# Paced units, and the two sums of a gate as accumulating transfers, in a fused linear-attention and MoE kernel

## The chip, the cores and the metric

The kernel runs on one core of one Trainium2 chip. The time is the device time of one execution in microseconds (us); lower is better. A core has five engines with a queue each, worked off in order: TensorE (PE; its weight loads are PEld), VectorE (DVE), ScalarE (ACT), GpSimd (POOL) and SyncE (SP). SP and POOL issue the transfers, which 16 DMA engines carry out.

## The reference

`q, k, v, a_re, a_im` have the shape (4, 8, 768, 48). For each of the 32 pairs of batch and head a complex state S (48 x 48) is carried over 768 steps, and its output goes through a mixture of eight experts.

```python
mag = np.sqrt(a_re * a_re + a_im * a_im)
scale = np.minimum(mag, 0.999) / (mag + 1e-06)
a_re_n, a_im_n = a_re * scale, a_im * scale
for t in range(S):
    ar, ai = a_re_n[:, :, t, :, None], a_im_n[:, :, t, :, None]
    new_re = ar * S_re - ai * S_im
    new_im = ar * S_im + ai * S_re
    S_re, S_im = new_re + einsum('bhd,bhe->bhde', k[:, :, t], v[:, :, t]), new_im
    y[:, :, t] = einsum('bhd,bhde->bhe', q[:, :, t], S_re)
...
x = y.transpose(0, 2, 1, 3).reshape(3072, 384)
do_compute = x @ w_skip > 0
# of the rows kept: expert e = argmax(x @ w_gate), gate_w its softmax weight
out[row] = x[row] + gate_w[row] * (np.maximum(x[row] @ w1[e], 0) @ w2[e])
# the other rows: out = x
```

## The kernel before

The 768 steps are cut into 6 chunks of 128 (`NCH`), the chunks into 3 groups of 2 (`NG`). In a group the 128 partitions hold two halves of a chunk (one runs backwards from the chunk's middle, one forwards), two chunks and 32 heads, so that one instruction serves them all.

**Gate** (`gate`, `scale`, `scale_last`). For a piece `i` of 8 of a half chunk's 64 steps (24 pieces, 8 a group, the last of a group with one step more) `a_re` and `a_im` are loaded into `ain` (four buffers) by eight transfers on SP. `scale` finds the factor that `mag` calls for: ScalarE squares both parts into `sq` (two buffers), VectorE adds the two squares (line 261), ScalarE takes Ln and Exp, VectorE forms max(l, 0) + t (line 265), ScalarE takes the last Exp, whose result is `t` (two buffers). Two VectorE products (lines 315 and 323) and a copy with changed sign on ScalarE (line 320) put the scaled `a` back into `ain`; small memsets on POOL set edge values. The last piece of all goes through `scale_last`, which has other steps.

**Chain** (`chain`). For each of a group's 65 steps two dependent VectorE instructions multiply the running product by the step's `a`: four products X (line 370), and their sums W (line 379). Each needs the one before. `cpos` counts the steps; the first of a group is a copy (line 364).

**Consume** (`consume`, `final` for the last piece). From W come weighted keys and queries `nw` and `iw` (lines 442 and 469, shared buffers, two). VectorE has five instructions for a piece, ScalarE a Square, Ln and Exp, PE four matmuls `sw`. In groups 0 and 2 PE transposes them and ScalarE copies them to `qk`; in groups 0 and 1 POOL writes some to DRAM (`kq`, line 491), for group 1 all of them (`spilled`), to be read back as `nat`.

**Unit** (`units`, `unit_at`, `unit`). For each chunk `c` and batch `b` (24 units, 8 a group): PE makes the scores `pa` of 8 heads, VectorE masks them (line 609, two instructions), the state `T` is moved on by the factor F (line 621 on VectorE, lines 632, 633 and 652 on PE), PE makes the output (lines 663, 666, 671), ScalarE copies it to `xa`, SP stores it. The scores of the next unit are issued within the present one. After the four units of a chunk a route (`route`) chooses the experts by some twenty small VectorE instructions and scatters the rows to `xs` by four indirect transfers on POOL. `weights`, `fetch`, `tokens` and `moe` then compute the experts.

**Order.** `Order` plans the sequence in which all this is written down. Each of the above is a generator that yields its VectorE time and a delay; the one with the lowest number of those that are ready goes next (`P_UNIT` 0.5, `P_ROUTE` 0.7, `P_CONSUME` 1, `P_GATE` 2, `P_WEIGHTS` 3), and a chain takes turns with them by `SHARE` and `CREDIT`. A delay is an estimate of when another engine will be done. When the program is built, a scheduler with a model of times orders each engine's instructions; what is written earlier goes first among those that the model has ready. `issue_after` pins an instruction behind another one. A gate may begin when the chain is within `AHEAD` = 2 pieces of its piece, and only after the gate before; units of a group begin when all of its pieces are consumed, beside the next group's chain (those of the last group after it).

Of the kernel before, what the change touches and what calls it, by code (L numbers as in the profile page):

```python
# [13 lines left out]
AF = mybir.ActivationFunctionType  # L14
ALU = mybir.AluOpType
# [4 lines left out]
B, H, S, D = 4, 8, 768, 48  # L20
# [3 lines left out]
HC = 64  # L24
NCH = S // C
NG = NCH // 2
# [14 lines left out]
P_UNIT, P_ROUTE, P_CONSUME, P_REST, P_GATE, P_WEIGHTS = 0.5, 0.7, 1, 1, 2, 3  # L41
# [2 lines left out]
CREDIT = 600.0  # L44
SLACK = 0.6
AHEAD = 2
FILL = 4


class Order:  # L50
# [22 lines left out]
    def add(self, prio, gen, delay=0.0):  # L73
        self.s.append([prio, self.t + delay, gen])
# [24 lines left out]
def vt(n, f=1.0):  # L99
    return (n / f + 65) / 0.96  # L100
# [8 lines left out]
class Kern:  # L109
# [140 lines left out]
    def scale(self, i, n, ain):  # L250


        V, A, o = self.nc.vector, self.nc.scalar, self.order
        sq = self.gt.tile([128, 2, n, D], F32, name=f"sq_{i}", tag="sq")
        t = self.gt.tile([128, n, D], F32, name=f"t_{i}", tag="t")
        N = n * D
        A.activation(sq.rearrange("p c j d -> p j c d"), ain[:, :, 0:2], AF.Square, scale=1.0 / 0.999)
        u, l = sq[:, 0], sq[:, 1]
        yield o.wait(0, o.act(2 * N, 1, o.t + (2500 if i else 6000)))
        with self.tc.issue_after(self.cins) if self.cpos else ExitStack():  # L260
            V.tensor_tensor(u, sq[:, 0], sq[:, 1], ALU.add)
        A.activation(l, u, AF.Ln, bias=self.tinym)
        A.activation(t, l, AF.Exp, scale=-0.5, bias=self.lnw, accum_out=self.acc[:, 1, i:i + 1])
        yield o.wait(vt(N), o.act(2 * N, 3, o.t + vt(N)))
        V.scalar_tensor_tensor(u, l, 0.0, t, ALU.max, ALU.add)
        A.activation(t, u, AF.Exp, scale=-0.5, accum_out=self.acc[:, 0, i:i + 1])
        yield o.wait(vt(N), o.act(N, 2, o.t + vt(N)))
        return t
# [32 lines left out]
    def gate(self, g, p):  # L301
        nc = self.nc
        V, A = nc.vector, nc.scalar
        n = LP + (1 if p == NP - 1 else 0)
        i = g * NP + p
        if i == 0:
            self.load_a(0)
        if i + 1 < NPC:
            self.load_a(i + 1)
        ain = self.ain[i]  # L310
        last = i == NPC - 1
        t = yield from (self.scale_last if last else self.scale)(i, n, ain)
        N = n * D
        o = self.order
        V.scalar_tensor_tensor(ain[:, :, 0], ain[:, :, 0], self.sgn, t, ALU.mult, ALU.mult)
        if p == 0:
            nc.gpsimd.memset(ain[0:64, 0, 0], 0.0)
        if n > LP:
            nc.gpsimd.memset(ain[64:128, LP, 0], 0.0)
        A.activation(ain[:, :, 2], ain[:, :, 0], AF.Copy, scale=-1.0)  # L320
        self.ready[i] = o.act(N, 1, o.t + vt(N))
        yield vt(N), 0
        V.tensor_tensor(ain[:, :, 1], ain[:, :, 1], t, ALU.mult)
        if p == 0:
            nc.gpsimd.memset(ain[0:64, 0, 1], 1.0)
        if n > LP:
            nc.gpsimd.memset(ain[64:128, LP, 1], 1.0)
        yield vt(N), 0
        self.gates_done = i + 1

    def gates(self):
        for g in range(NG):
            for p in range(NP):
                if FILL <= g * NP + p <= FILL + E:
                    self.late(g * NP + p - FILL)
                while self.cpos < (g * NP + p - AHEAD) * LP:
                    yield 0, 200
                yield from self.gate(g, p)

    def chain(self, g):  # L340
        V = self.nc.vector
# [4 lines left out]
        prev = None  # L346
        for p in range(NP):
            i = g * NP + p
            while self.gates_done <= i:
                yield 0, 100  # L350
            yield self.order.wait(0, self.ready[i])
            num, inv = self.load_qk(i)
# [347 lines left out]
    def units(self, g):  # L700
        self.nat(2 * g, 0)
        self.nat(2 * g, 1)
        self.unit_at(2 * g, 0)
        for cc in range(2):
            c = 2 * g + cc
            while self.routes_done < c - 1:
                yield 0, 200
            if c > 0:
                yield from self.make_F(c - 1)
            if not self.last(c):  # L710
                self.lg = self.rt.tile([128, B, H // 2, E + 1], F32, name=f"lg_{c}", tag="lg", bufs=2)
            self.xa = self.rt.tile([128, B, XW], F32, name=f"xa_{c}", tag="xa", bufs=2)
            self.nc.gpsimd.tensor_copy(self.xa[:, :, DM], self.tok[:, :, c])
            for b in range(B):
                yield from self.unit(c, b)
                self.units_done += 1
            if not self.last(c):
                self.routes.append((self.lg_t, self.route(c, self.lg, self.xa)))
# [153 lines left out]
    def attention(self):  # L872
        with ExitStack() as ctx:
# [11 lines left out]
            for t in self.vts + self.sts:  # L885
                nc.gpsimd.memset(t[:, :, D:64], 0.0)
            self.pr_ins, self.T2, self.ain, self.QK, self.Ew, self.T, self.pa, self.W, self.ready, self.nats, self.kqt = [{} for _ in range(11)]
            self.cpos = self.gates_done = self.cons_done = self.routes_done = self.units_done = 0
            self.rx_t = 0.0
            self.cq, self.routes = [], []  # L890
            o = self.order = Order()
# [347 lines left out]
```

## Time and profile before

| | |
|---|---|
| three runs | 530.79, 538.38, 548.51 us; median 538.38 |
| profiled execution | 534.78 us, span 533.0 us |
| busy PE, PEld | 425.7 us (80%), 371.0 us (70%) |
| busy DVE, ACT, POOL | 411.9 us (77%), 293.3 us (55%), 88.3 us (17%) |
| mean granted PE clock | 0.896 of full speed |
| moved | 85.72 MB in 160523 packets, mean 161 GB/s |

All views are of one execution. A row of instructions has its line, engine and operation, the tile written and those read, the count and the times; behind `<-` in a row of waits stands what ended the wait, then the total in us, how often, and the longest. The strips show the busy share of 40 equal slices in tenths. A row that begins with a stretch `A:B` has the busy time of each engine in it with the number of instructions, then the granted PE clock as a share of full speed, the busy share of the DMA engines, and GB/s; asked for one line alone, the busy times are that line's. PE's busy time is modelled, and a busy PE isn't PE at its peak.

### The profile page before, as it was taken

How to read it: one execution, taken by the hardware profiler on the slowest of the kernel's cores; microseconds unless marked ns; L12 is line 12 of the kernel's file. 1: busy time of each engine (PE TensorE's matmuls, PEld its weight loads, DVE VectorE, ACT ScalarE, POOL GpSimd, SP SyncE). 2: the span in 40 equal slices, each digit the busy share in tenths (PEclk: the TensorE clock that was granted, in tenths of full speed). 3: DMA queues.
4: the chain of work that ended last, by engine and by line, in shares of the span. 5: the costliest groups of instructions: out<-in, count | busy, mean ns of one | idle time of the engine just before them, and what ended most of it. 6: DMA issues, size and time to landing. Idle time of an engine off the chain costs nothing. (4 is left out here: it accounts for less than half of the span.)

```text
span 533.0 us, 10037 instructions
## 1 busy us (share of the span) xinstructions
PE 425.7 (80%) x3253; PEld 371.0 (70%) x3253; DVE 411.9 (77%) x1139; ACT 293.3 (55%) x658; POOL 88.3 (17%) x158
## 2 busy tenths in 40 slices
PE   0355545579999223799999998999999999999994
PEld 0233323468887101688878788998998999999994
DVE  2998899966998999889889848899479666866621
ACT  3657667724557555578878665432266545564420
POOL 4011111101122274000000300221211001211111
PEclk9986876577999665599999999999999999999998
DMA  4557866788878767866735515744669567656300
GB/s 86 115 110 168 196 149 159 166 158 192 227 184 205 189 168 181 178 140 154 158 83 122 139 37 164 213 110 122 209 221 302 176 235 244 215 190 216 101 20 28
DMA packets 160523, 85.72 MB, mean 161 GB/s; under 512 B 134491, under 2 KB 154463, under 8 KB 160464
## 3 DMA queue, kind: packets, MB, share of 16 engines
q1 hardware_dynamic: 155216, 70.93, 52.4%
q0 software_dynamic: 5248, 14.07, 9.1%
q8 instruction: 28, 0.46, 0.4%
q14 instruction: 31, 0.25, 0.2%
HBM read 61.84 MB, written 25.21 MB: 163 GB/s over the span
## 5 line engine op out<-in xcount | busy, mean ns | idle before, releaser
L451 PE MATMUL sw<-ws,ident 128*128 128x384 f32 x84 | 46.1, 686 | 40.5 <-ACT ws L437 40.5
L370 DVE TENSOR_TENSOR X<-W,ain 128x192 f32<-128x192 f32 x192 | 68.0, 354 | 3.6 <-ACT ain L320 0.3
L929 DVE TENSOR_TENSOR l<-r,h 128x768 fp32r<-128x768 f32 (+1 forms) x56 | 58.1, 1070 | 11.8 <-ACT h L928 11.7
L928 ACT CAST h<-r 128x768 fp32r<-128x768 f32 (+1 forms) x56 | 49.6, 924 | 22.1 <-DMA r<-in_moe_w_dram 17.0
L451 PEld LDWEIGHTS sw<-ws,ident 128*128 128x128 f32 x84 | 19.8, 262 | 54.2 <-issue 27.8
L993 PE MATMUL ph<-xh,h 128*128 128x256 f32 x192 | 53.0, 282 | 0.6 <-issue 0.6
L993 PE MATMUL ph<-xh,l 128*128 128x256 f32 x192 | 53.2, 282 | 0.0
L995 ACT ACTIVATE hh<-ph 128x256 fp32r<-128x256 f32 x64 | 23.7, 382 | 53.0 <-PE ph L993 52.9
L379 DVE TENSOR_TENSOR W<-X 128x96 f32<-128x96 f32 x192 | 48.9, 255 | 3.2
L993 PE MATMUL ph<-xl,h 128*128 128x256 f32 x192 | 51.0, 281 | 0.0
L532 PE MATMUL tp<-ident,iw 128*96 128x128 f32 x128 | 23.7, 332 | 33.1 <-DVE iw L469 32.8
L996 DVE SCALAR_TENSOR_TENSOR hl<-ph,hh 128x256 fp32r<-128x256 f32 x64 | 25.5, 419 | 28.2 <-ACT hh L995 28.2
L539 ACT COPY qk<-tp 96x256 f32<-96x256 f32 x128 | 39.9, 369 | 13.1 <-PE tp L532 12.9
L609 DVE TENSOR_TENSOR at<-pa,mask 128x512 f32<-128x512 f32 x48 | 32.8, 686 | 18.1 <-PE pa L589 18.0
L1016 PE MATMUL po<-h,hh 128*128 128x384 f32 x128 | 43.8, 342 | 0.0
L532 PEld LDWEIGHTS tp<-ident,iw 128*96 128x96 f32 x128 | 16.7, 151 | 38.5 <-issue 30.6
L1017 PE MATMUL po<-l,hh 128*128 128x384 f32 x128 | 43.3, 338 | 0.0
L732 POOL DMA_INDIRECT xs<-xa,sl x24 | 28.6, 1192 | 85.3 <-DVE l L929 24.2
L663 PE MATMUL py<-at,vt 128*64 128x128 f32 x384 | 42.0, 291 | 0.0
L1018 PE MATMUL po<-h,hl 128*128 128x384 f32 x128 | 39.5, 337 | 0.0
L589 PE MATMUL pa<-qk 96*128 96x128 f32 x256 | 37.3, 297 | 0.1
L993 PEld LDWEIGHTS ph<-xh,h 128*128 128x128 f32 x192 | 36.2, 189 | 0.8 <-issue 0.8
(225 smaller groups left out, 1070.6 us busy)
## 6 DMA issues: line engine op xcount, KB each, us to landing
r<-in_moe_w_dram SPq DMA_DIRECT2D x24, 512.0 KB, 5.2
r<-in_moe_w_dram SPq DMA_DIRECT2D x32, 384.0 KB, 4.3
nat<-kq SPq DMA_DIRECT2D x8, 768.0 KB, 5.5
kq<-nw POOLq DMA_DIRECT2D x24, 192.0 KB, 3.7
kq<-iw POOLq DMA_DIRECT2D x24, 192.0 KB, 3.1
vt<-in_v_dram SPq DMA_DIRECT2D x24, 192.0 KB, 3.0
out_dram<-xa SPq DMA_DIRECT2D x24, 192.0 KB, 2.3
ain<-in_a_re_dram SPq DMA_DIRECT2D x90, 48.0 KB, 2.8
```

Source lines behind the costliest of these rows:

```text
L370: V.tensor_tensor(X, prev.unsqueeze(1).to_broadcast([128, 2, 2, D]), windows(ain[:, j]), ALU.mult)
L379: self.cins = V.tensor_tensor(W[:, j, ::-1], X[:, :, 0], X[:, :, 1], ALU.add).ins
L451: nc.tensor.matmul(sw, self.ident, ws[:, :, c], start=(c == 0), stop=(c == 1))
L532: nc.tensor.transpose(tp[:, jj], src[:, s * 4 + jj], self.ident)
L539: nc.scalar.copy(o, tp[:, :, :, cc].rearrange("p j s b -> p b s j"))
L663: PE.matmul(py[j * 64:j * 64 + 64, hp], vt_[:, 2 * hp + j], at[:, 2 * hp + j], start=True, stop=(c == 0))
L928: nc.scalar.copy(hi[:, ks], raw)
L929: nc.vector.tensor_tensor(lo[:, ks], raw, hi[:, ks], ALU.subtract)
L993: pe = PE.matmul(ph, w[:, k, js], x[:, k], start=(n == 0), stop=(n == len(terms) - 1))
L1016: PE.matmul(po, hh[:, j, sl], w2h[:, j], start=(j == 0), stop=False)
L1017: PE.matmul(po, hh[:, j, sl], w2l[:, j], start=False, stop=False)
L1018: pe = PE.matmul(po, hl[:, j, sl], w2h[:, j], start=False, stop=(j == NF - 1))
```

## The change

There are three parts. In `scale`, pieces 3 to 22 (`SUMS` = 3) form both sums by transfers that POOL issues and that add to their destination, instead of by VectorE; a Relu on ScalarE takes the place of the max, and the planner is told of 3500 ns for each. `gates` no longer runs a gate to its end before the next: it adds each to the plan as an entry of its own, and the set `gated` takes the place of the count `gates_done`. In `units`, unit number n of a group (n = 0 to 7) isn't begun before the next chain has done 7n steps (`PACE` = 7); the units of the last group wait for the end of the last chain.

```diff
+SUMS = 3
+PACE = 7
...
     def scale(self, i, n, ain):
...
         A.activation(sq.rearrange("p c j d -> p j c d"), ain[:, :, 0:2], AF.Square, scale=1.0 / 0.999)
         u, l = sq[:, 0], sq[:, 1]
+        if i >= SUMS:
+            add = lambda x, y: self.nc.gpsimd.dma_start(x, y, accum_op=ALU.add)
+            add(u, l)
+            A.activation(l, u, AF.Ln, bias=self.tinym)
+            A.activation(t, l, AF.Exp, scale=-0.5, bias=self.lnw, accum_out=self.acc[:, 1, i:i + 1])
+            A.activation(l, l, AF.Relu)
+            yield 0, o.act(5 * N, 6) - o.t + 3500
+            add(l, t)
+            A.activation(t, l, AF.Exp, scale=-0.5, accum_out=self.acc[:, 0, i:i + 1])
+            yield 0, o.act(N, 2) - o.t + 3500
+            return t
         yield o.wait(0, o.act(2 * N, 1, o.t + (2500 if i else 6000)))
...
     def gate(self, g, p):
...
-        self.gates_done = i + 1
+        self.gated.add(i)
...
     def gates(self):
...
                 while self.cpos < (g * NP + p - AHEAD) * LP:
                     yield 0, 200
-                yield from self.gate(g, p)
+                self.order.add(P_GATE, self.gate(g, p))
+                yield 0, 0
...
     def chain(self, g):
...
-            while self.gates_done <= i:
+            while i not in self.gated:
                 yield 0, 100
...
     def units(self, g):
...
             for b in range(B):
+                while self.cpos < min((g + 1) * (HC + 1) + (cc * B + b) * PACE, NG * (HC + 1)):
+                    yield 0, 100
                 yield from self.unit(c, b)
```

More of the change, by code (lines that the diff above doesn't have):

```diff
@@ L887, in attention @@
             self.pr_ins, self.T2, self.ain, self.QK, self.Ew, self.T, self.pa, self.W, self.ready, self.nats, self.kqt = [{} for _ in range(11)]
-            self.cpos = self.gates_done = self.cons_done = self.routes_done = self.units_done = 0
+            self.gated = set()
+            self.cpos = self.cons_done = self.routes_done = self.units_done = 0
             self.rx_t = 0.0
```

## The prediction

> **What bounds the kernel now.** First the page: span, busy engines, and the strip for DMA.
>
> ```profile
> span 533.0 us, 10037 instructions
> PE 425.7 (80%) x3253; PEld 371.0 (70%) x3253; DVE 411.9 (77%) x1139; ACT 293.3 (55%) x658; POOL 88.3 (17%) x158
> DMA  4557866788878767866735515744669567656300
> ```
>
> No engine is full over the span, so I cut it at the three chains. The first copy of a chain (line 364) dates them: the last of the three stands at 195.3, and each chain's last W step ends shortly before the next one's work takes over. I take 24 to 95.4 for chain 0 (after the start-up), 95.4 to 205.2 for chain 1, 205.2 to 306.5 for chain 2, then the last units, then the experts. Columns are length, busy time of PE, PEld, DVE, ACT and POOL with counts, granted PE clock, DMA share, GB/s.
>
> ```profile
> L364 DVE COPY W<-ain x3: 204/205/209, 12.0 to 195.3; 128x96 f32<-128x96 f32 x3
> 24.00:95.40 71.40, 38.29 (x142) 25.55 (x140) 66.02 (x177) 48.43 (x128) 9.46 (x19) 0.76 0.71 158
> 95.40:205.20 109.80, 75.27 (x579) 61.24 (x578) 95.71 (x284) 58.58 (x134) 30.93 (x45) 0.78 0.79 186
> 205.20:306.50 101.30, 94.37 (x729) 74.88 (x730) 88.25 (x246) 71.19 (x169) 7.55 (x11) 0.89 0.63 141
> 388.00:533.00 145.00, 135.50 (x960) 134.24 (x958) 89.33 (x152) 68.55 (x123) 21.07 (x25) 0.98 0.54 178
> ```
>
> Chain 0 is VectorE's: 66.0 of 71.4 us. Chain 1 has 14.1 us of VectorE idle time and takes 38 us more than chain 0. Chain 2 is shared by PE (94.4 of 101.3) and VectorE (88.3). The experts are PE's, and the change doesn't touch them. In chain 1 the loss has a place; the second row of each pair below counts the W steps alone.
>
> ```profile
> 110.00:165.00 55.00, 54.48 (x463) 47.34 (x464) 43.62 (x120) 25.96 (x59) 8.87 (x15) 0.88 0.80 188
> 110.00:165.00 55.00, 6.31 (x25) 0.88 0.80 188
> 165.00:205.00 40.00, 14.40 (x87) 9.09 (x85) 38.15 (x123) 24.19 (x53) 20.30 (x27) 0.69 0.78 188
> 165.00:205.20 40.20, 7.39 (x29) 0.69 0.79 189
> DVE at L609 <- PE pa L589: 7.8, 5, 3.8
> DVE RX L621 <- ACT T L659: 1.8, 1, 1.8
> DVE sq L265 <- ACT t L263: 2.8, 4, 1.6
> ```
>
> From 110 to 165 PE is full with the eight units of group 0, and the chain makes 25 steps in 55 us (2.2 us each); afterwards it makes 29 in 40.2 us (1.4) with PE a third busy. The waits of VectorE in chain 1 are mainly for a unit's scores (7.8 us) and its state (1.8). The last row is chain 0's: the wait for the first Exp ahead of a gate's second sum.
>
> **The change part by part.**
>
> *Two sums off VectorE.* Line 261 counts the gates in each stretch; the timeline of VectorE (start, duration) prices a sum.
>
> ```profile
> 24.00:95.40 71.40, 3.91 (x7) 0.76 0.71 158
> 95.40:205.20 109.80, 4.48 (x8) 0.78 0.79 186
> 205.20:306.50 101.30, 2.75 (x5) 0.89 0.63 141
> 39.49 0.55 DVE L261 TENSOR_TENSOR sq<-sq 128x384 f32<-128x384 f32 x1
> 39.96 0.95 DVE L442 TENSOR_TENSOR nw<-num,W 128x768 f32<-128x768 f32 x1
> 41.21 0.26 DVE L379 TENSOR_TENSOR W<-X 128x96 f32<-128x96 f32 x1
> 41.51 0.36 DVE L370 TENSOR_TENSOR X<-W,ain 128x192 f32<-128x192 f32 x1
> 46.63 0.25 DVE L379 TENSOR_TENSOR W<-X 128x96 f32<-128x96 f32 x1
> 46.80 0.55 DVE L323 TENSOR_TENSOR ain<-ain,t 128x384 f32<-128x384 f32 x1
> ```
>
> A sum holds the engine from 39.49 to 39.96, 0.47 us. But it is a filler between dependent steps: W followed by its own X takes 41.21 to 41.51, 0.30 us; with a filler behind it the engine is free again after 46.63 to 46.80, 0.17. So about 0.12 us of each sum is hidden now, and taking it out gives 0.35, or 0.70 a gate. Chain 0: 7 gates, 4.9 us, and the 2.8 us of waits at line 265 go with the instruction. Chain 1: 8 gates, 5.6. Chain 2: 5 gates, 3.5 at most; PE is 93% busy there, so I count half, 1.8. What is late next is line 315, which waits for `t`, now behind two transfers.
>
> *Units one by one.* The work of a unit doesn't change: eight score products and the other matmuls, the copies on ScalarE, on SP a load of `vt`, one of `nat` and a store of `out`, and after four units a route with four scatters on POOL. In chain 1 all of it moves from 25 steps to 56 (eight units, 7 steps apart), past loads of `ain`, `num` and `inv` on SP that keep their number. PE's 75.3 us fit beside a chain of 95, and the scores of unit b+1 are issued with unit b, 7 steps before they are read: I take away the waits for scores and state, 9.6 us, and keep the other 4.5 us of idle time. For chain 2 the row of line 609 counts the score instructions that fall inside it:
>
> ```profile
> 205.20:306.50 101.30, 8.27 (x12) 0.89 0.63 141
> ```
>
> Twelve are six units of the eight, over the chain's 65 steps, so more than 7 steps apart already; the limit moves little: 0. The units of group 2 wait for the chain's end either way.
>
> VectorE alone would then need 71.4 - 4.9 - 2.8 = 63.7 us for chain 0 and 109.8 - 5.6 - 9.6 = 94.6 for chain 1, together 158.3 instead of 181.2.
>
> *Forty accumulating transfers.* Nothing like them is in this trace, so bounds. They move 192 KB from SBUF to SBUF on POOL's queue. The nearest rows are POOL's own 192 KB writes to DRAM; and the SP queue's best stretch, with the experts' weights.
>
> ```profile
> kq<-iw POOLq DMA_DIRECT2D x7, 192.0 KB, 2.7
> kq<-nw POOLq DMA_DIRECT2D x7, 192.0 KB, 3.6
> q0 software_dynamic: 734, 2.61, 15.3%
> kq<-iw POOLq DMA_DIRECT2D x15, 192.0 KB, 3.4
> kq<-nw POOLq DMA_DIRECT2D x16, 192.0 KB, 3.9
> 400.00:420.00 20.00, 18.72 (x135) 18.50 (x135) 15.14 (x33) 12.49 (x20) 2.41 (x3) 1.00 0.74 247
> ```
>
> In chain 0, 14 writes (2.61 MB) take 15.3% of 71.4 us: 0.78 us of all 16 engines each. At the rate of 400 to 420 (0.74 of 20 us for 4.94 MB, 3.0 us a MB) 192 KB would be 0.59. An addition has to read what it adds to as well, so up to twice: 0.59 to 1.56, never below nothing. I take 1.0, the middle in ratio, since no row is nearer. Chains 0 and 1 hold 30 of them. Their DMA work now is 0.71 x 71.4 + 0.79 x 109.8 = 137.4 us of all 16 engines; with 30 it is 167.4. That is more than VectorE's 158.3: **the transfers become the later end in the two chains.** By 0.59 the sum is 155.1 and VectorE decides, by 1.56 it is 184.2 and nothing is left. The Trainium skill (DMA: Bandwidth & Descriptors, Rules for kernel authors) says that an accumulating transfer reads its destination and writes it later; by that rule the price lies towards the upper end, which no row here can show.
>
> In time, a transfer lands 2.7 to 3.9 us after its issue, and POOL's issue is in order: behind an addition that waits for ScalarE stand the `kq` writes, whose landing frees `nw` and `iw`, and the memsets of `ain`. POOL is busy 9.5 of 71.4 us, so I put 0 on its time.
>
> *ScalarE.* One Relu a gate, 0.53 us by the row of line 266, 3.7 us in chain 0: 52 of 64, hidden while it isn't full. The waits for landings are the rival below.
>
> ```profile
> L266 ACT ACTIVATE t<-sq 128x384 f32<-128x384 f32 (+1 forms) x6 | 3.2, 528 | 3.2 <-DVE sq L265 3.2
> L257 ACT ACTIVATE sq<-ain 128x768 f32<-128x768 f32 (+1 forms) x7 | 6.0, 854 | 15.0 <-DMA num<-in_k_dram 8.9 <-DMA ain<-in_a_im_dram 6.1
> ```
>
> *Two gates under way.* No instruction is added; loads of `ain` may be issued up to a piece earlier. `sq` and `t` have two buffers, so two gates is all that there is room for. I count 0: what it hides is the two landings.
>
> **The sum.** Chains 0 and 1: 181.2 to 167.4, with 1 us for uneven queues 168.4: -12.8. Chain 2: -1.8. Rest 0. Together -14.6. The profiled execution took 534.8 us, its span and 1.8 around it, and becomes 520.2; the median of the runs shown is 538.4, 3.6 above it, and on that scale the forecast is **524**.
>
> **The rivals.**
>
> *VectorE stays the end* (an addition costs 0.59). Then 158.3 and some 2 us of new waits at line 315: -20.9 - 1.8 = -22.7, or 515.7 on the median's scale. For it: the strip of DMA shows slices of 6 and 7 beside those of 8, so there is room. Against: a second read is needed.
>
> *The additions cost 1.56.* 184.2 instead of 181.2, less 1.8: 539.6 on the median's scale, no change. For it: the shares of 0.71 and 0.79 now. Against: some of that traffic (the zero rows, `nat`) can move.
>
> *ScalarE waits for the landings* (the slower side). Ln and the second Exp stand in ScalarE's queue behind a transfer that the Square and the Relu have to start. If the order leaves too little work between, the engine stands still, and behind it the copies of `qk`, for which PE's transposes wait, and the Ln and Exp of the consume step, for which line 461 on VectorE waits. A gate of chain 0 has 71.4 / 7 = 10.2 us; ScalarE is busy 48.4 / 7 = 6.9 of these, 7.4 with the Relu. So it decides in chain 0 from 1.4 us of standing per addition. With one Square's worth of other work between (0.85), a landing of 3.6 leaves 2.75, twice a gate: 12.9 us a gate, +19.1 in chain 0; in chain 1 58.58 / 8 + 0.53 + 5.5 = 13.4 a gate, 106.8, -3.0; in chain 2 71.2 + 5 x 6.03 = 101.3, 0. Together +16.1: 554.5 on the median's scale. For it: the Squares of chain 0 stand 15.0 us for loads, so landings do come later than the order expects. Against: ScalarE's queue has work of other pieces that can lie between.
>
> *A colder PE.* With units spread, PE isn't full, and rows with a half-busy PE have a lower clock.
>
> ```profile
> 200.00:220.00 20.00, 8.53 (x20) 4.38 (x21) 19.56 (x58) 10.29 (x26) 6.50 (x8) 0.50 0.79 191
> ```
>
> Chain 1's 75.3 us at a mean clock of 0.78 are 117.4 at 0.50: 7.6 us more than the chain takes now; with up to 7.7 gained in chain 0 and 1.8 in chain 2 the time is 536 to 544 on the median's scale, no change. The Trainium skill (TensorE: Matmul & The Clock Gate, Part 1) says that idle stretches of some 3.4 us halve the clock; by that rule gaps between paced units would do it, and the row agrees for sparse work (0.50). But 0.78 was granted in a chain 1 whose last 40 us had PE a third busy at 0.69, so a PE that is three quarters busy should get more.
>
> *The change doesn't do what it says*: instructions are ordered when the program is built, and the units might bunch again or the sums wait for one another. It would look like no change, and I count it there.
>
> **How the numbers follow.** Forecast (-14.6) 0.45, VectorE the end 0.2, dear additions or no effect 0.17, ScalarE 0.13, a cold PE 0.05. The executions before lie between 530.8 and 548.5, so about 2% (10.8 us) is what a measurement here can tell from no change. Of the forecast's 0.45 some 0.33 lies beyond 10.8 us and 0.11 within; so faster 0.33 + 0.2 = 0.53, no change 0.11 + 0.17 + 0.05 = 0.33, slower 0.13 and a remnant, 0.14. The range goes from 508, below the case of VectorE (515.7) by what the lowest run before lies under the median (7.6), to 541, past the case of dear additions; ScalarE's 554 and little more is left out. The forecast's own range is 515 to 530.
>
> **What would show it.**
>
> ```profile
> q0 software_dynamic: 5248, 14.07, 9.1%
> ```
>
> No instruction of lines 261 and 265 after the third gate. The DMA share from 24 us to the end of chain 1 near 1.0 and the software queue's share of the span (row above) up by some 7 points, 40 us in 533; if by less than 5, VectorE is the end. Steps of chain 1 even, near 1.5 us, no stretch of 2.2, and the waits at line 609 nearly gone. The third chain's first copy at about 182 instead of 195.3. ScalarE's waits for the `sq` transfers under 1.4 us each. The forecast is wrong if those waits are longer, if additions take more than 1.3 us of the 16 engines, or if chain 2 lengthens because PE gets its units late.

## The result, and the profile after

The changed kernel takes **553.26 us** in the median (550.22 to 567.27), the kernel before 542.06 in the runs beside it: a ratio of **1.031**, 95% interval 1.023 to 1.038. (Some executions of any kernel here run a few per cent slower than the rest, those behind the profiles of repin and two_late below among them; ratios are taken from the others alone, so this one isn't 553.26 / 542.06.) It is slower, and the forecast of 524 was wrong. The profiled execution has a span of 552.1 us, 19.1 more than before; by the ratio the loss is some 17 us. The rows of the page that answer to those of before:

```profile
span 552.1 us, 10087 instructions
PE 422.7 (77%) x3253; PEld 367.3 (67%) x3253; DVE 396.6 (72%) x1099; ACT 302.6 (55%) x678; POOL 124.0 (22%) x198
PE   0053643549998641599999998999998999999994
DMA  4678888789999989898875425634659568656200
q0 software_dynamic: 11008, 22.04, 17.5%
```

VectorE is busy 15.3 us less (411.9 before), 0.38 for each of the 40 sums that went. The transfers are fuller: the software queue takes 17.5% of 552.1 us instead of 9.1% of 533.0, so 48 us of all 16 engines more, 1.20 for each addition (the packets of the other large queue take 279 us in both). Busy time fell as meant, and the kernel is slower.

Where the 19.1 us arose is dated by two kinds of instruction: a chain's first copy (line 364 before, 379 after), and the masking of a unit's scores (609 before, 624 after), of which this view counts those after 200 us, so the units of groups 1 and 2.

```profile
L364 DVE COPY W<-ain x3: 204/205/209, 12.0 to 195.3; 128x96 f32<-128x96 f32 x3
...
L609 DVE TENSOR_TENSOR at<-pa,mask x32: 668/686/693, 227.5 to 367.0; 128x512 f32<-128x512 f32 x32
```

```profile
L379 DVE COPY W<-ain x3: 201/202/210, 21.5 to 218.6; 128x96 f32<-128x96 f32 x3
...
L624 DVE TENSOR_TENSOR at<-pa,mask x32: 653/682/693, 240.1 to 382.0; 128x512 f32<-128x512 f32 x32
```

The first chain begins 9.5 us later (12.0 to 21.5). The first unit of group 1 begins 12.6 us later (227.5 to 240.1). From there to the last unit's copy of x (376.3 before, 391.2 after) it is PE that works, in both kernels:

```profile
227.50:376.30 148.80, 146.76 (x1422) 125.49 (x1422) 124.27 (x421) 91.30 (x222) 14.51 (x18) 1.00 0.54 135
```

```profile
240.10:391.20 151.10, 145.52 (x1418) 124.83 (x1419) 121.30 (x420) 90.72 (x220) 20.54 (x24) 1.00 0.59 144
```

PE is busy 146.8 of 148.8 us, and 145.5 of 151.1. The experts follow: 156.7 us before, 160.9 after. So the 19.1 are 12.6 of a later first unit, 2.3 in that stretch, and 4.2 in the experts. **What the first 230 us are worth is mainly the date at which PE gets the units of group 1**; a shorter chain that doesn't move it is worth little.

The path to that date is in both traces: the last consume step of group 1 (its `iw`), POOL's writes to `kq`, the reads back to `nat`, PE's transposes `tu`, the scores. First before, then after:

```profile
208.09 0.94 DVE L469 TENSOR_TENSOR iw<-inv,W 128x768 f32<-128x768 f32 x1
213.98 1.95 SPq L502 DMA_DIRECT2D nat<-kq  x2
219.63 1.91 PE L517 MATMUL tu<-ident,nat 128*96 128x128 f32 x8 [2.77 <-DMA nat<-kq]
```

```profile
222.12 0.94 DVE L484 TENSOR_TENSOR iw<-inv,W 128x768 f32<-128x768 f32 x1
228.92 0.38 SPq L517 DMA_DIRECT2D nat<-kq  x1
235.74 1.04 PE L532 MATMUL tu<-ident,nat 128*96 128x128 f32 x8
```

The last consume step begins 7.3 us after the last chain step of chain 1 before, and 7.5 after, so in these two the date follows the chain's end (in some of the variants below it doesn't). It begins at 208.1 before and at 222.1 after: 9.5 from the first step, 5.6 from chain 0 (81.6 to 87.2 us from its first copy to its end), 1.4 less from chain 1, 0.3 behind it. The windows of after, cut within 3 us of its own chain ends (108.7 and 214.6; columns as before):

```profile
24.00:107.50 83.50, 39.11 (x134) 25.30 (x135) 63.77 (x171) 51.53 (x129) 22.06 (x33) 0.72 0.80 171
107.50:217.50 110.00, 77.03 (x594) 62.09 (x592) 88.22 (x259) 61.26 (x143) 41.56 (x60) 0.78 0.93 210
```

VectorE has 19.7 us of idle time in the first row (5.4 in chain 0 before) and 21.8 in the second. What it waited for in chain 0, and what ScalarE did:

```profile
L329 DVE SCALAR_TENSOR_TENSOR ain<-ain,col,t 128x384 f32<-128x384 f32 (+1 forms) x7 | 4.4, 623 | 13.1 <-ACT t L270 5.2 <-DMA num<-in_k_dram 5.1 <-DMA ain<-in_a_re_dram 2.8
L476 DVE TENSOR_TENSOR ws<-sw,ws 128x384 f32<-128x384 f32 x7 | 3.9, 552 | 3.5 <-ACT ws L474 3.4
```

```profile
ACT t L270 <- DMA sq<-t: 10.2, 4, 3.6
ACT sq L265 <- DMA sq<-sq: 7.1, 5, 2.8
```

The first product of a gate (line 329, which was 315) waits 13.1 us in all. The row puts 5.2 of them down to the factor `t` and the rest to loads; but in the timeline each of the five waits ends within 0.1 us of the end of the Exp that writes `t`, so all are put down to `t` here. ScalarE stands 17.3 us for the landings.

Chain 1 is another matter. The masking of group 0, and the longest waits of VectorE in its window, in the changed kernel:

```profile
L624 DVE TENSOR_TENSOR at<-pa,mask x16: 676/680/691, 125.9 to 172.3; 128x512 f32<-128x512 f32 x16
DVE X L385 <- ACT ain L334: 4.5, 2, 4.3
DVE nw L457 <- DMA kq<-nw: 3.3, 1, 3.3
DVE at L624 <- PE pa L604: 0.6, 1, 0.6
```

The waits for scores that the prediction took away did go, from 7.8 to 0.6 us. Others stand in their place: the chain waits for a gate's copy with changed sign, and `nw` for the landing of a `kq` write.

### The profile page after: what moved, and what is told of

Its sections match the earlier page's. It is cut to its first block, busy times and chain, and to the rows that moved or that the text cites. A ratio compares the mean times of both kernels' runs of the same rounds, so it can differ in the third digit from the quotient of the medians.

```text
span 552.1 us, 10087 instructions
## 1 busy us (share of the span) xinstructions
PE 422.7 (77%) x3253; PEld 367.3 (67%) x3253; DVE 396.6 (72%) x1099; ACT 302.6 (55%) x678; POOL 124.0 (22%) x198
## 3 DMA queue, kind: packets, MB, share of 16 engines
q0 software_dynamic: 11008, 22.04, 17.5%
## 4 chain that ended last, share of the span: by engine, by line
PE 52%; DMA 17%; DVE 11%; issue 8%; ACT 5%; SPq 4%; POOL 1%; DVEq 0%; POOLq 0%; ACTq 0%
PE ph L1012 10%; PE pa L604 5%; SPq L228 4%; PE py L678 4%; PE sw L466 4%; PE px L686 4%; PE ps L667 4%; PE po L1035 3%; PE po L1036 3%; PE po L1037 3%; PE py L681 3%; DMA xg<-xs 2%; PE tp L547 2%; DMA inv<-in_k_dram 2%; PE tu L532 2%
## 5 line engine op out<-in xcount | busy, mean ns | idle before, releaser
L466 PE MATMUL sw<-ws,ident 128*128 128x384 f32 x84 | 44.5, 668 | 56.0 <-ACT ws L452 56.0
L947 ACT CAST h<-r 128x768 fp32r<-128x768 f32 (+1 forms) x56 | 49.6, 924 | 20.9 <-DMA r<-in_moe_w_dram 13.1
L678 PE MATMUL py<-at,vt 128*64 128x128 f32 x384 | 40.4, 288 | 0.0
L604 PE MATMUL pa<-qk 96*128 96x128 f32 x256 | 35.4, 285 | 2.4 <-DVE at L624 2.0
L1041 POOL DMA_INDIRECT out_dram<-og,idx x16 | 16.0, 997 | 92.8 <-DVE og L1040 56.5
```

Source lines behind the costliest of these rows:

```text
L466: nc.tensor.matmul(sw, self.ident, ws[:, :, c], start=(c == 0), stop=(c == 1))
L604: nc.tensor.matmul(pa[h // 4][:, h % 4], KT(h), QT(h), start=True, stop=True)
L678: PE.matmul(py[j * 64:j * 64 + 64, hp], vt_[:, 2 * hp + j], at[:, 2 * hp + j], start=True, stop=(c == 0))
L947: nc.scalar.copy(hi[:, ks], raw)
```

## The experiments

The kernel before ran beside each on the same chip. "First score" is the start of group 1's first masking, "last unit" the last copy of x. Chain 0 is taken from its first copy to its last step, chain 1 from there to its own last step. A dash means that there is no such number on record, or that it isn't used. Each profile is of one execution: that of the kernel before is of one of 534.8 us, where its medians beside the experiments are 538.7 to 540.5, so a few us between two traces may be chance.

| run | ratio (95%) | chain 0, 1 begin to end | first score | last unit | span |
|---|---|---|---|---|---|
| before | 1 | 81.6, 107.3 | 227.5 | 376.3 | 533.0 |
| changed | 1.031 (1.023-1.038) | 87.2, 105.9 | 240.1 | 391.2 | 552.1 |
| pace | 1.002 (0.998-1.006) | 82.7, 115.0 | 235.5 | 382.9 | 539.6 |
| pin | 1.006 (1.001-1.010) | 81.6, 110.4 | 232.2 | 377.8 | 538.2 |
| sums | 1.038 (1.028-1.049) | 88.9, 112.0 | 240.5 | 396.3 | 556.3 |
| two | 1.018 (1.007-1.028) | 80.8, 98.9 | 230.7 | 383.6 | 543.3 |
| two_start | 0.995 (0.990-0.999) | 85.9, 99.9 | 226.7 | 375.1 | 533.9 |
| start | 1.045 (1.034-1.056) | 91.3, 103.5 | 243.6 | 399.1 | 560.3 |
| extra | 1.018 (1.012-1.025) | 84.4, 111.4 | 239.8 | 384.4 | 546.2 |
| nowait | - | 81.6, 94.4 | 240.9 | 402.1 | 563.5 |
| sums_nowait | 1.043 (1.037-1.048) | 89.4, 100.8 | 248.0 | 401.0 | 561.8 |
| pool | 1.023 (1.016-1.029) | 86.1, 102.3 | 235.4 | 391.8 | 551.1 |
| pool_two | 1.015 (1.010-1.020) | 87.2, 102.4 | 235.9 | 388.2 | 548.1 |
| sums_late | 0.994 (0.991-0.998) | 82.5, 106.2 | 226.7 | 373.6 | 534.1 |
| est500 | 1.038 (1.033-1.044) | 89.1, 112.2 | 243.4 | 395.8 | 555.5 |
| repin | 1.027 (1.021-1.034) | - | - | - | - |
| repin_start | 1.043 (1.035-1.051) | 89.3, 105.1 | 240.2 | 396.2 | 556.0 |
| both | 1.044 (1.038-1.050) | 88.2, 119.3 | 250.2 | 402.4 | 562.5 |
| both_nowait | 1.037 (1.031-1.042) | 83.7, 101.7 | 243.1 | 388.4 | 549.3 |
| two_late | 1.004 (1.000-1.008) | - | - | - | - |

From the first score to the last unit it is 145 to 161 us in all of them; the runs at or under 1.006 have their first score at 235.5 or earlier, all others but one (two, 230.7) at 235.4 or later. The stretch from there is not the same in all: it is 144.6 to 153.0 us where the granted PE clock in it was 1.00, and 161.2 in nowait, where it was 0.95.

### The three parts, one at a time

**Pacing alone.**

```diff
-SUMS = 3
+SUMS = 99
...
-                self.order.add(P_GATE, self.gate(g, p))
-                yield 0, 0
+                yield from self.gate(g, p)
```

> The pacing of the units alone; gates one after the other, both sums on VectorE. If the accumulating transfers are the whole loss (landings waited for on ScalarE and VectorE, and the start held up), this is 5 to 10 us faster than before: chain 1's 9.6 us of waits of VectorE for scores and state go, the chain starts at 12 us, the DMA share in chain 1 stays near 0.8. If the paced units are what costs (work that comes late and is missing later), it is 5 us or more slower, and the loss shows after the third chain's first copy.

540.59 us, no change. The limit is written, but the units of group 0 aren't spread. The masking of group 0, before, and with pacing alone:

```profile
L609 DVE TENSOR_TENSOR at<-pa,mask x16: 679/686/693, 108.0 to 157.8; 128x512 f32<-128x512 f32 x16
```

```profile
L623 DVE TENSOR_TENSOR at<-pa,mask x16: 677/684/692, 109.2 to 164.0; 128x512 f32<-128x512 f32 x16
```

Worked out from the trace, the units begin at chain steps 77, 78, 79, 82, 86, 89, 94, 98 with pacing, and at 77, 78, 79, 82, 86, 89, 95, 97 without. By the code the planner can't write the fourth to the eighth unit before steps 86, 93, 100, 107 and 114; but the order of instructions is made afterwards, when the program is built, by what is ready, and in it they stand earlier again.

**Pacing that holds.** The masking tied behind the chain step at which the plan has it:

```diff
+            with self.tc.issue_after(self.cins) if c < 2 else ExitStack():
```

> The pacing alone, and the masking of a unit's scores in group 0 pinned on VectorE behind the chain's step at which the plan writes it, so that the pacing holds in the instruction order too (in the run with pacing alone the eight units stood at steps 77 to 98, as before, though the plan begins them at 75 to 114). If the pacing is worth what was forecast once it takes hold, chain 1 is 8 to 10 us shorter than 107.3 and the waits for scores fall from 10 us to 2. If PE then gets the units too late, the chain is shorter and the time isn't.

```profile
L624 DVE TENSOR_TENSOR at<-pa,mask x16: 678/682/692, 108.1 to 180.6; 128x512 f32<-128x512 f32 x16
L624 DVE TENSOR_TENSOR at<-pa,mask 128x512 f32<-128x512 f32 x16 | 10.7, 684 | 7.4 <-PE pa L603 7.4
```

Now they are spread, to 180.6 us, and the wait for the scores is still 7.4 us (7.8 before). Chain 1 takes 110.4 us, not less than 107.3, and the ratio is 1.006. So spreading the units does not by itself take the waits away. In the changed kernel, where the built order has them at steps 79 to 107, only 0.6 us of them are left; which of its parts does that isn't shown, and it gained nothing, since VectorE's idle time in chain 1 is 21.8 us there, and 14.1 before.

**The transfers alone** (`PACE = 0`, gates one after the other).

> The accumulating transfers alone; gates one after the other, units not paced. If the landings are the loss, it is slower than before by 10 us or more: a gate then holds the next one up for its two landings of 4 to 5.5 us, so line 329 makes VectorE wait more than the 13 us of chain 0 in the changed kernel. If the full DMA engines are the loss instead, chain 0 (share 0.80 in the changed kernel) is no longer than before and only chain 1 is. If pacing or two gates is what costs, it is within 3 us of before or faster.

558.48 us, 1.038: the whole loss, and more, comes with them. Chain 0 grows from 81.6 to 88.9 us. Line 329 stands 8.7 us in it, less than the 13 or more that were expected of a loss by landings.

**Two gates alone**, and two gates **after the first three**:

```diff
-                self.order.add(P_GATE, self.gate(g, p))
-                yield 0, 0
+                if g * NP + p < 3:
+                    yield from self.gate(g, p)
+                else:
+                    self.order.add(P_GATE, self.gate(g, p))
+                    yield 0, 0
```

> Two gates under way alone; both sums on VectorE, units not paced. If the late start (first chain step at 21.5 instead of 12.0 us) comes from three gates being planned at once, it is here too: slower by some 9 us. If it comes from the first accumulating transfer, which stands in POOL's queue ahead of the small memsets of the first gate, the start is at 12 us here and the time within 3 us of before.

> Two gates under way alone (sums on VectorE, no pacing), with gates 0 to 2 one after the other. In the run with two gates alone the chain began 9.4 us late and chains 1 and 2 took 98.9 and 98.4 us instead of 107.3 and 105.0. If the late start is a loss of its own, this is 7 to 9 us faster than that run, so about as before or some 2 us faster. If PE sets the end from the third chain on, the two shorter chains are given back after chain 2 (84.1 us there instead of 70.5) and the time is that of before, 0 to -2 us. If the gain of the two chains lasts, it is 10 us faster.

The first chain's first copy (first and last of three), two gates alone, and with the first three in turn:

```profile
L379 DVE COPY W<-ain x3: 201/201/209, 21.4 to 188.1; 128x96 f32<-128x96 f32 x3
```

```profile
L382 DVE COPY W<-ain x3: 201/203/210, 11.9 to 185.6; 128x96 f32<-128x96 f32 x3
```

The late start belongs to the two gates and not to the transfers: gates 0 to 2 are all let in at step 0, and the engines do parts of the second and third ahead of the first chain step. Alone it costs 1.8%; without it two gates under way give 0.995. Their chains 1 and 2 are 99.9 and 95.9 us (107.3 and 105.0 before), 16 us less together (chain 0 is 4.3 longer), but the first score moves by 0.8 us only, to 226.7, and the gain with it: from there PE sets the end. The last consume step of group 1 does come 4.0 us earlier (204.1). Of these, 1.6 go between the last write to `kq` and the reads back, and 1.7 between PE's first transposes and the first score; why is not settled.

**The whole change without the late start.**

> The whole change, but with gates 0 to 2 one after the other and only the later ones added as entries of their own. Both accounts of the late start (three gates planned at once; the accumulating transfer ahead of the memsets) give a first chain step near 12 us and 7 to 10 us less than the changed kernel, so about 2% slower than before stays at most. If the start is slack that the later chains take up, the time is that of the changed kernel.

1.045, not better. The first copy is at 11.9 again, but chain 0 takes 91.3 us, and the first score comes at 243.6. The 9.5 us are in the changed kernel's trace, but here they didn't come out by themselves: with the gates in turn another order is built, and it loses them elsewhere.

### What it is in the transfers

**Their load.** The kernel before, with 40 accumulating transfers of 192 KB into two tiles that nothing reads:

```diff
+        if 2 <= i < 22:
+            x = self.extra[(2 * i + k) % 2]
+            self.nc.gpsimd.dma_start(x, W[:, 4 * k:4 * k + 4]..., accum_op=ALU.add)
```

> The kernel before, with forty more accumulating transfers of 192 KB that read W and add to a tile that nothing reads, two for each piece, so that the DMA engines carry the load of the changed kernel and nobody waits for a landing. If the load on the DMA engines is what costs in the changed kernel, it is 8 us or more slower than before, with chain 1 at a share above 0.9. If it is the wait for the landings, it is within 5 us of before.

```profile
q0 software_dynamic: 11008, 21.94, 17.9%
```

1.018: VectorE and PE never wait for them in the trace, ScalarE for 0.2 us, and 40 transfers cost 1.8%, some 10 us. That is their load together with their issue on POOL, which stands in one queue with the writes to `kq`. Chain 0 is 2.8 and chain 1 4.1 us longer.

**Their landing.** The additions read the squared imaginary part and go to tiles that nothing reads; Ln, Exp and Relu go on from the squared real part, at once, so the imaginary part is left out of the scale. First in the changed kernel, then with the transfers alone.

> The changed kernel, with each of the forty additions read from the square of the imaginary part and added to a tile that nothing reads; Ln, Exp and Relu go on from the square of the real part at once, so the imaginary part is left out of the scale and no engine waits for a landing. Same transfers, same instructions on ScalarE, no sums on VectorE. If the landings are the loss, the idle time of VectorE in chain 0 falls from 20 to below 10 us and the time by 8 us or more against the changed kernel. If it is the load on DMA and POOL, or the late start, it stays within 3 us of the changed kernel.

> The transfers alone, but each adds to a tile that nothing reads, so nobody waits for its landing; Ln, Exp and Relu go on from the squared real part, and the imaginary part is left out of the scale. Load, issue time and VectorE's savings stay. Theory 'the landing': chain 0 falls from 88.9 to some 80, DVE idle in it from 18 to under 10; what is left is the load, which cost 1.8% where VectorE had not been relieved, less the 14 us taken from VectorE of which some 5 count: 540 to 546 us, a ratio of 1.00 to 1.015. Theory 'the load': as with the waits, 555 to 560, 1.03 to 1.04.

Neither expectation of nowait holds: it takes 570.11 us in the median and 564.51 at the lowest, well more than the changed kernel. sums_nowait is at 1.043, no better than with the waits and just past the range of 'the load'. But the chains did get shorter: chains 0 and 1 together by 17.1 us in nowait (81.6 and 94.4), by 10.7 in sums_nowait (89.4 and 100.8, against 88.9 and 112.0). The time goes between the chain's end and the first score:

| run | chain 1 ends | last `iw` of group 1 | steps of chain 2 ahead of it | first score |
|---|---|---|---|---|
| before | 200.8 | 208.1 | 5 | 227.5 |
| changed | 214.6 | 222.1 | 2 | 240.1 |
| nowait | 198.3 | 216.5 | 11 | 240.9 |
| sums | 212.9 | 220.8 | 4 | 240.5 |
| sums_nowait | 202.3 | 224.1 | 12 | 248.0 |

Chain 1 ends in nowait 2.5 us earlier than before the change, and the first score comes 13.4 us later: group 1's last consume step begins 18.2 us after the chain's end instead of 7.3, with 11 steps of the next chain ahead of it instead of 5, and the way from there to the score is 5 us longer. So these two runs do not say that the landings cost nothing. Without them the chains are shorter, and in the built order the gain doesn't reach the work that PE waits for. Why the order comes out so isn't shown.

**No transfer at all.** The same sums by POOL's own instruction:

```diff
-            add = lambda x, y: self.nc.gpsimd.dma_start(x, y, accum_op=ALU.add)
+            add = lambda x, y: self.nc.gpsimd.tensor_tensor(x, x, y, ALU.add)
```

> The run of the transfers alone (1.038), with each of its 40 additions done by POOL's own elementwise instruction instead of a transfer: VectorE is rid of the same sums, ScalarE keeps the same instructions, no transfer is added and nothing lands late. An addition on POOL is estimated at 0.5 to 1.2 us, from its 128x386 memset (427 ns) and its 128x192 select (367 ns). Theory 'the landing' (a gate's chain through ScalarE is longer by two landings of 4 to 5.5 us, and that sends VectorE's saved time into waits): the waits of chain 0 fall back and 14 us of sums stay off VectorE, so 530 to 536 us, a ratio of 0.985 to 0.997. Theory 'the load' (1.2 us of all DMA engines each) gives the same here. Theory 'another order' (a sum taken from VectorE lets the build order the rest less well, whatever does the sum): 1.02 to 1.04.

> Two gates under way after the first three, no pacing (the best version so far, 0.995), and its sums from the fourth gate on done by POOL's own instruction. If VectorE's sums are what the chains wait for, chains 1 and 2 lose 3 to 5 us more: 526 to 532, a ratio of 0.975 to 0.988. If PE sets the end from the middle of chain 1 on, as with two gates alone (shorter chains given back after them), nothing comes of it: 534 to 540, 0.99 to 1.0.

1.023, and 1.015 with two gates. The range that theories 'the landing' and 'the load' gave, and both ranges for pool_two, missed; 'another order' (1.02 to 1.04) holds in pool by its number. (pool_two also tells the planner 1200 ns instead of 3500.) The idle time did go: VectorE stands 5.9 and 3.2 us in chains 0 and 1, each over its whole length, instead of 17.9 and 23.3 in sums. But its own instructions got slower. X before, and with the sums on POOL:

```profile
L370 DVE TENSOR_TENSOR X<-W,ain x192: 322/355/360, 12.3 to 304.2; 128x192 f32<-128x192 f32 x192
```

```profile
L384 DVE TENSOR_TENSOR X<-W,ain x192: 341/357/2075, 12.2 to 317.5; 128x192 f32<-128x192 f32 x192
L384 DVE TENSOR_TENSOR X<-W,ain 128x192 f32<-128x192 f32 x192 | 79.1, 412 | 5.8 <-ACT ain L334 1.5
...
L263 POOL TENSOR_TENSOR sq<-sq 128x384 f32<-128x384 f32 (+1 forms) x20 | 27.7, 1385 | 31.6 <-ACT sq L259 31.2
```

The median of X is the same, the longest is 2075 ns instead of 360. The timeline says which: the 163 X that overlap no sum on POOL last 341 to 361 ns, and every longer one is among the 29 that do. A sum on POOL takes 1.3 to 1.4 us in the mean, where 0.5 to 1.2 was expected. So pool removes the landings and brings a cost of its own, and doesn't decide between the theories.

**Where they stand.** Transfers only for the gates from the seventeenth on (`SUMS = 16`), whose pieces are all of chain 2; and the same with two gates:

> The transfers alone, but only for the gates from the seventeenth on: 14 additions, all for the third chain, where the DMA share before is 0.63 and PE is the busiest engine; the other gates keep their sums on VectorE. Theory 'the landing': chains 0 and 1 as before (81 to 83 and 105 to 110), chain 2 not shorter because PE sets the end there: 536 to 544, 0.995 to 1.007. Theory 'so much a transfer' (the 3.8% divided among 40, whichever engine waits): 14/40 of it, 1.013, 545 to 548.

> Two gates under way after the first three (0.995), no pacing, and the sums by transfers only for the gates from the seventeenth on (0.994 by itself). If the two gains add up: 0.985 to 0.992, 531 to 535. If both are the same slack in front of PE, which is full from chain 2 on: 0.993 to 0.998, 536 to 539. If the product's place costs here as in chain 0 (no tie for these gates): 1.00 to 1.01.

0.994: the fourteen transfers for chain 2 cost nothing, where 1.013 would be their share. They are issued from 182.7 to 267.2 us, eight of them ahead of the first score (226.7). So the loss comes from the gates of chains 0 and 1. By the spans, 13.0 of the 23.3 us of sums arise ahead of the first score, 7.0 between it and the last unit, 3.3 in the experts. The two small gains don't add up (1.004).

**The place of the products.** With the sums gone from VectorE, the products of a gate in chain 0 (lines 329 and 337) stand 6 to 9 chain steps (sums) or 8 to 16 (the changed kernel) ahead of the piece that needs them, against 3 to 5 before; with the sum, its tie to a chain step (`issue_after`, line 274 of the changed kernel) has left the gate. So VectorE might wait for `t` only because it asks too early. The products were tied again, first line 329 alone:

```diff
-            yield 0, o.act(5 * N, 6) - o.t + 3500
+            yield 0, o.act(5 * N, 6) - o.t + 500
...
+        with self.tc.issue_after(self.cins) if i >= SUMS and self.cpos else ExitStack():
```

> The transfers alone (1.038), with the planner's estimate of an addition 500 instead of 3500 and the product of line 329 tied behind the chain step at which the plan has it, which by that estimate is 4 steps ahead of its piece, as in the kernel before. Theory 'the product stands too early': its 8.8 us of waits in chain 0 and 1.8 in chain 1 go, chain 0 falls from 88.9 to 77 to 82, chain 1 from 112 to 102 to 107, and the time to 532 to 543, a ratio of 0.985 to 1.005. Theory 'the landing': a Square, two landings and four activations take longer than the 14.7 us that there are, and the wait moves to the product's new place or to the chain step behind it: 550 to 560, 1.02 to 1.04.

> The whole change (1.031), with the product tied behind the chain step at which the plan has it, 5 to 8 steps ahead of its piece, where the built order had 8 to 12; nothing else differs. 'Too early': of the 13.1 us of waits at line 329 in chain 0 under 3 are left, chain 0 goes from 87.2 to 77 to 81 and the time to 541 to 546 (the late first step, 9.5 us, stays), 1.00 to 1.012. 'The landing': 550 to 556, 1.02 to 1.035.

> The whole change with the first three gates one after the other (1.045), the product held until 5 steps ahead of its piece and tied behind the chain step there. 'Too early': chain 0 from 91.3 to 76 to 81, chain 1 from 103.5 to 98 to 103, and with the first step at 11.9 a time of 526 to 537, 0.975 to 0.995; if PE sets the end from the second chain on, the upper end of it. 'The landing': 550 to 562, 1.02 to 1.045.

1.038, 1.027 and 1.043, as without the tie. But these tied one product, and the other stood ahead and took the wait over (8.6 us in chain 0 of est500). With both tied, the transfers kept, and then with nobody who waits for a landing:

> est500 with both products of a gate tied behind the chain step, 3 to 5 steps ahead of the piece in chain 0, as in the kernel before. 'Too early': no waits at lines 330 and 339 in chain 0, chain 0 at 77 to 82 and the time at 532 to 545, 0.985 to 1.01. 'The landing': the waits move on to what ScalarE does after a landing (the chain's copy, the consume step's line 476), chain 0 stays at 86 to 90 and the time at 552 to 562, 1.02 to 1.04.

> As both, but each transfer adds to a tile that nothing reads, so that nobody waits for its landing; Ln, Exp and Relu go on from the squared real part, and the imaginary part is left out of the scale. 'Too early': the same as both within 1%. 'The landing': chain 0 at 76 to 80 and 8 to 15 us less than both, 1.00 to 1.015, what is left being the load (1.8% where VectorE was not relieved). 'The load': as both, 1.02 to 1.04.

The waits of VectorE in chain 0, of both, then of both_nowait:

```profile
DVE ws L477 <- ACT ws L475: 8.1, 3, 3.7
DVE ain L330 <- ACT t L270: 4.1, 2, 3.5
```

```profile
DVE ws L477 <- ACT ws L475: 11.2, 6, 4.3
```

**That theory falls too**: 1.044 and 1.037. The products stand 3 to 5 steps ahead again, and the wait has moved on, to the consume step's line 477, which needs ScalarE. And where ScalarE waits for no landing (both_nowait), line 477 waits no less in chain 0, while ScalarE stands 16.6 us at the Squares for loads. Chain 1 is 17.6 us shorter there (101.7 against 119.3), but as in the other two runs without landings the last consume step of group 1 comes late, 20.7 us after the chain's end and behind 12 steps of chain 2 (9.3 us and 6 steps in both). Its `iw`:

```profile
218.28 0.95 DVE L485 TENSOR_TENSOR iw<-inv,W 128x768 f32<-128x768 f32 x1
```

**What is shown and what isn't.** Shown: the change to the gates of chains 0 and 1 is the loss (sums 1.038 against sums_late 0.994), and the late first step comes from two gates under way (two against two_start). Transfers that nobody waits for cost 1.8% in the kernel before (extra). What the landings cost isn't settled: both against both_nowait is 0.7%, with intervals that overlap, and sums_nowait is no faster than sums; in all three pairs the chains get shorter without them, and the last consume step of group 1 comes late. The place of the products isn't it. If the 1.8 and the 0.7 add up, 2.5 of the 4.4% in `both` are named, and the rest stays open. It goes with a relieved VectorE and another built order, and no run separates the two. The experts' 4.2 us stay open too: all variants but pace are 2.1 to 5.1 us longer there, the two fastest among these. No version here beats the kernel before by the 2% that the prediction set as the least that a measurement can tell; two_start and sums_late are half a per cent faster.

## Why the prediction was wrong, point by point

- **The step that failed** is the sum for chains 0 and 1, 181.2 to 168.4 us. It took VectorE's sums and waits off, put the transfers in as work of the 16 engines, and let the larger of the two be the time; it had no term for waits that come in place of those removed, and 0 for two gates and for POOL's time. By the marks of the table the two chains went from 188.9 to 193.1 us instead, with 19.7 and 21.8 us of idle time of VectorE in their windows for 5.4 and 14.1, and the first step came 9.5 us late. The runs tie the longer chains to the gates with transfers and the late step to the two gates; how much of the former is landing, load or order stays open in part.
- **What bounds the kernel.** The prediction cut the span at the chains and asked which engine is full in each. It didn't ask what the first two chains are for. The row for 227.5 to 376.3 could have been asked for: PE is full from group 1's first score on, so a gain ahead of it counts as far as it moves that date. two_start shortens chains 1 and 2 by 16 us, with 4.3 more in chain 0, for half a per cent.
- **Two sums off VectorE**, 0.35 us each. Right in size (0.38 of busy time), wrong in worth: VectorE's idle time in chain 0 rose from 5.4 to 19.7 us. The prediction named line 315 as late next and gave it no price in its forecast; it took 13.1 us.
- **Units one by one**, 9.6 us. The waits went (at the masking 7.8 to 0.6 us, for the state 1.8 to none), and the gain did not come, since other waits took their place in chain 1. By itself the part does nothing: the built order undoes it (pace), and where it holds, the waits for scores stay at 7.4 us (pin). "The change doesn't do what it says" was a rival, and for this part alone it was true.
- **The price of an accumulating transfer.** 1.0 us of the 16 engines was taken, 1.20 measured, between the bounds. By 1.20 the DMA work of chains 0 and 1 is 0.80 x 83.5 + 0.93 x 110 = 169 us, where 167.4 was worked out. So this term was right, and the conclusion from it was not: the transfers were to be at a share near 1.0 in the two chains, and the share is 0.80 in chain 0 and 0.93 in chain 1. A sum of work is a lower bound, and here neither VectorE nor the transfers reached it. The Trainium skill (DMA: Bandwidth & Descriptors, Rules for kernel authors) says that an accumulating transfer reads its destination and writes it later. It gives no price; the 1.20, against 0.78 for a plain write of the same size (to DRAM), goes with it.
- **Two gates under way**, 0. Wrong: +1.8% alone, and with it a first step 9.4 us later, without which it is 0.995. The prediction looked at the buffers and at what is hidden, and not at the start, where three gates are let in at once.
- **POOL's time**, 0. What it costs isn't shown: the issues take 0.9 us each (last section), and POOL is busy 124.0 us instead of 88.3. The case that the prediction named is in the trace once: `nw` waits 3.3 us in chain 1 for the landing of a `kq` write, which POOL issued right behind an addition.
- **ScalarE waits for the landings**, the rival at 554.5, came out nearest, with the right name and the wrong working. It was to decide from 1.4 us of standing for an addition; 17.3 us for 14 additions in chain 0 are 1.24. It gave +19.1 in chain 0 where 5.6 came, and of the total only 0.7% comes back with the landings taken out (both_nowait). That its total is near 553.26 is chance.
- **VectorE stays the end** and **dear additions** need a price of 0.59 or 1.56; neither was measured. **A colder PE**: 0.78 in chain 1 before and after, and a mean of 0.896 and 0.891; it didn't come.
- **What would show it.** The third chain's first copy was to move from 195.3 to 182 and stands at 218.6; the software queue's share rose by 8.4 points for the 7 expected; the waits at the masking nearly went, as expected. Of the three signs of being wrong at most one came: ScalarE's waits are 1.24 us an addition in the mean, with single ones up to 3.6; an addition takes 1.20, and chain 2 is no longer than before. None of the three watched VectorE's next waits or the start.

## What to carry to other kernels

Find the date from which one engine is full to the end, follow the path of work that sets it (here the last consume step of a group, a write, a read back and the transposes), and price a change by how far it moves that date, not by the waits that it removes ahead of it. Work taken from an engine in a chain of dependent steps can come back as waits at the next late producer, so name that producer and give it a price. A shorter chain can also run ahead of the work that the full engine waits for, as in the runs without landings; and where the program's order is made at build time, read the built order before counting on a plan's pacing. Parts that look independent should be timed alone and together: pacing 1.002, two gates 1.018 and the transfers 1.038 gave 1.031 as one.

## What the runs showed of the hardware

An accumulating transfer of 192 KB from SBUF to SBUF costs 1.20 us of the 16 DMA engines (1.23 in extra), against 0.78 for a write of that size to DRAM, and POOL issues it in 0.9 us. The issues (mean ns behind the busy time), and the landings in chain 1 of the changed kernel:

```profile
L263 POOL DMA_DIRECT2D sq<-sq x20 | 18.6, 930 | 58.6 <-ACT sq L259 41.0 <-DVE ain L337 12.9 <-DMA num<-in_q_dram 3.4
L263 POOL DMA_DIRECT2D sq<-t x20 | 18.3, 914 | 50.7 <-ACT sq L267 50.6
```

```profile
sq<-t POOLq DMA_DIRECT2D x7, 192.0 KB, 4.9
sq<-sq POOLq DMA_DIRECT2D x6, 192.0 KB, 5.6
```

In the median they land 4.9 and 5.6 us after the issue there, where the `kq` writes of chain 1 took 3.4 and 3.9 before.

POOL's elementwise sum of two tiles holds up VectorE: with 40 of them (pool), VectorE is busy 427.8 us instead of 411.9 though it has 40 instructions fewer, and its longest X is 2075 ns. The Trainium skill (SBUF — State Buffer, SBUF: two separate sides) says that VectorE with two SBUF inputs and GpSimd share a pair of ports under an exclusive lock, and the one that comes second stands still for a whole instruction. The trace agrees in that X takes longer than 361 ns only where it overlaps a sum on POOL, and then up to 2075 ns, with the median unchanged.
